# Attention and SwiGLU on one core: from pairs of heads over 112 keys to fours of heads over 64 keys, and a first batch in two passes

## The chip, the cores and the metric

The kernel runs on one core of one Trainium2 chip. The metric is the device time of one execution in microseconds (us). Shown are the median of three runs of the kernel before, and one further execution that was taken by the hardware profiler. A core has five engines that each work through their own list in order: TensorE (PE in the profile, with its weight loads as PEld), VectorE (DVE), ScalarE (ACT), GpSimd (POOL) and SyncE (SP). PE writes to PSUM[...].

## The reference

Attention over 8 batches, 12 heads, 448 tokens and head width 64, then a SwiGLU block over the 3584 tokens with width 768 and inner width 1536. All inputs and the output are fp32; the kernel works in fp16 with fp32 sums.

```python
scores = (q @ k.transpose(0, 1, 3, 2)) / 8.0          # 8 x 12 x 448 x 448
attn = softmax(scores)                                # over the keys
x = (attn @ v).transpose(0, 2, 1, 3).reshape(3584, 768)
g = x @ w_gate
out = (g * sigmoid(g) * (x @ w_val)) @ w_out          # 3584 x 768
```

## The kernel before, in words

**Attention.** The unit is a pair of heads, 48 pairs in all, six to a batch. A token index is split as four tokens a partition over 112 partitions (`P = 112`, `NC = 4`), so that a load moves runs of four tokens. `load_qk16` and `load_v` bring q, k and v in through POOL's DMA queue, which casts fp32 to fp16 on the way; pair 0 comes as fp32 through SP's queue (`load_qk32`). q and k must be turned so that the head width lies on the partitions. `prep` does that in two ways: for pairs under `NPE = 11` PE turns them (L208) and DVE copies the result (L209), and from pair 11 on POOL reorders (L167) and SP issues DMA transposes (L170, L174).

`qk(pr, c)` makes the scores of one chunk of 112 keys: two matmuls of 64 contraction rows and 128 columns, one per head, each over 448 queries (L217), which sit in the upper and the lower half of the array's rows. ACT takes the exponential of both heads at once, 112 x 896 numbers (L225). `pv_chunk` multiplies the exponentials with v, which carries a column of ones so that the sums of the softmax come along: 8 matmuls of 112 rows, 128 columns and 65 moving columns a chunk (L243, L251), 32 a pair. DVE divides (L262, L264), and `turn_x` turns the result into the layout of the next block, on PE for pairs under `XPE = 12` (L291, then L298 on DVE), by DMA afterwards (L300, L304). The last 64 queries of a batch are turned together in `turn_rests` (L310).

**Feed-forward.** A batch is a block of 384 or 512 tokens. `ffn1_steps` has 12 steps a block: six matmuls for the gate (L326 into `gp`), a tanh on ACT (L341), six matmuls for the value (`vp`), and two DVE operations (L345, L348). `ffn2_steps` has steps of 12 matmuls with 384 moving columns (L371), an ACT copy (L378) and the stores (L390). All weights are loaded once and stay in SBUF.

**Order.** The whole order is written out by hand under `tc.manual_schedule()`. A start stage runs the first `FIRST = 6` pairs, batch 0, to the end with little else beside them. Then a list of visits, `plan`, interleaves: each visit has the scores of two or three chunks, the products of at most one or two pairs, and some feed-forward steps of the batch that was finished before. `wq` says at which pair the weight loads are put into POOL's list, between the loads of q, k and v: `wg`, `wv` in four slices each, then `wo` in two halves. PSUM is split into three tiles of two banks (`ps_s`, scores and gates) and two banks (`ps_f`, everything else).

Of the kernel before, what the change touches and what calls it, by code (L numbers as in the profile page):

```python
# [16 lines left out]
HS = 4096.0  # L17
NB = 2
GP = 3
NPE = 11  # L20
LA = 6
RB = 5
FIRST = 6
WIDE = 8
XPE = 12
NE = 4
NX = 6
NV = 5
VS = 9
EB = 15  # L30
# [3 lines left out]
def kernel(  # L34
# [14 lines left out]
    P = 112  # L49
    NC = S // P  # L50
# [4 lines left out]
    NGRP = NPAIR // GP  # L55
    GPB = NHP // GP
    sm_scale = float(D) ** -0.5
    OH = DM // 2
    MQ = S - D
# [13 lines left out]
    load_table("exp_and_others")  # L73

    consts = ctx.enter_context(tc.tile_pool(name="consts", bufs=1))
    raws = ctx.enter_context(tc.tile_pool(name="raws", bufs=2))
# [5 lines left out]
    ps_f = ctx.enter_context(tc.tile_pool(name="ps_f", bufs=2, space=PSUM))  # L82

    Es = [consts.tile([P, NC * EB + 1, D], FP16, name=f"E{i}") for i in range(NE)]
    Xts = [consts.tile([128, 7, D], FP16, name=f"xt{i}") for i in range(NX)]
    Xrs = [consts.tile([D, 128], FP16, name=f"xr{i}") for i in range(3)]
    Vts = [consts.tile([P, 2, NC, D + 2], FP16, name=f"vo{i}") for i in range(NV)]
    vraw = consts.tile([P, VS, 2, NC, D], FP16, name="vraw")
# [11 lines left out]
    wo = [consts.tile([128, NFB, OH], FP16, name=f"wo{i}") for i in range(2)]  # L100
# [5 lines left out]
    def dummy(n):  # L106
        wp = ps_f.tile([128, 512], FP32, tag="f", name="wp")
        for _ in range(n):
            nc.tensor.matmul(wp[:], lhsT=warm[:, 0:128], rhs=warm[:], start=True, stop=True)  # L109

    def load_qk32(pr):
        rq = raws.tile([P, 2, NC, D], FP32, tag="rq", bufs=RB)
        rk = raws.tile([P, 2, NC, D], FP32, tag="rk", bufs=RB)
        for dst, src in ((rq, q), (rk, k)):
            nc.sync.dma_start(dst[:], src[0, 2 * pr : 2 * pr + 2].rearrange("h (p c) d -> p h (c d)", c=NC))
        raw[pr] = (rq[:], rk[:])

    pairbuf = []

    def load_qk16(pr, n=2):  # L120
        h0 = 2 * (pr % 2) if pr >= 14 else 0
        if h0 == 0:
            q16 = raws.tile([P, 4, NC, D], FP16, tag="rq", bufs=RB, name="q16")
            k16 = raws.tile([P, 4, NC, D], FP16, tag="rk", bufs=RB, name="k16")
            pairbuf[:] = [q16, k16]
        q16, k16 = pairbuf
        for dst, src in ((q16, q), (k16, k)):
            flat = src.rearrange("b h s d -> (b h) s d")[2 * pr : 2 * pr + 2 * n]
            nc.gpsimd.dma_start(dst[:, ds(h0, 2 * n)], flat.rearrange("h (p c) d -> p h (c d)", c=NC))  # L129
        for i in range(n):  # L130
            h = h0 + 2 * i
            raw[pr + i] = (q16[:, h : h + 2], k16[:, h : h + 2])

    def load_v(pr, n=1):
        b, h = divmod(2 * pr, H)
        nc.gpsimd.dma_start(  # L136
            vraw[:, ds(pr % VS, n)].rearrange("p r h c d -> p (r h) (c d)"),
            v[b, h : h + 2 * n].rearrange("h (p c) d -> p h (c d)", c=NC),
        )

    def copy_v(pr):
        nc.vector.tensor_copy(Vts[pr % NV][:, :, :, 0:D], vraw[:, pr % VS])  # L142

    def load_w(kind, i):
        if kind == "o":
            src = moe_w_out[:, ts(i, OH)].rearrange("(f p) m -> p f m", p=128)
            dst = wo[i]
        else:
            src = (moe_w_gate if kind == "g" else moe_w_val)[:, ts(i, DF // 4)].rearrange(
                "(t a p) m -> t p a m", p=128, t=2  # L150
            )
            for t in range(2):
                nc.gpsimd.dma_start(wgv[kind, i][:, ts(t, NCB // 2), :], src[t])
            return
        nc.gpsimd.dma_start(dst[:], src)

    def prep(pr):
        rq, rk = raw[pr]
        if pr == 0 or pr >= NPE:
            qk16 = attp.tile([P, 2, NC, 2, D], FP16, tag="qk16", bufs=3)  # L160
            for t, src in enumerate((rq, rk)):
                dst = qk16[:, 1 - t].rearrange("p c h d -> p h c d")
                if pr == 0:
                    nc.vector.tensor_copy(dst[:, 0], src[:, 0])
                    nc.scalar.activation(dst[:, 1], src[:, 1], AF.Copy)
                else:
                    nc.gpsimd.tensor_copy(dst, src)  # L167
        qkT[pr] = attp.tile([128, 2 * S + D], FP16, tag="qkT", name="qkT", bufs=5)
        if pr >= NPE:
            nc.sync.dma_start_transpose(  # L170
                qkT[pr][:, 0 : 2 * S].rearrange("p (c q) -> p c q", q=P),
                qk16[:].rearrange("p t c h d -> p (t c h d)"),
            )
            nc.sync.dma_start_transpose(  # L174
                qkT[pr][:, 2 * S :].rearrange("p (c q) -> p c q", c=1),
                qk16[0:D, 1, 0].rearrange("p h d -> p (h d)"),
            )
            return None

        def turn0():  # L180
            for t in range(2):
                tp = ps_s.tile([128, 2, 512], FP32, tag="s", name="tp")
                for c in range(NC):
                    for hx in range(2):
                        nc.tensor.matmul(
                            tp[ts(hx, 64), c // 2, ds(c % 2 * P, P)],
                            lhsT=qk16[:, 1 - t, c, hx],
                            rhs=ident[0:P, 0:P],
                            start=True,
                            stop=True,  # L190
                        )
                dst = qkT[pr][:, ts(1 - t, S)].rearrange("p (a x) -> p a x", a=2)
                nc.vector.tensor_copy(dst[:, 0], tp[:, 0, 0 : 2 * P])
                nc.scalar.activation(dst[:, 1], tp[:, 1, 0 : 2 * P], AF.Copy)
                if t == 0:
                    tq = tp
            nc.vector.tensor_copy(qkT[pr][:, 2 * S :], tq[:, 0, 0:D])

        def turn():
            if pr < FIRST + 2:  # L200
                tp = ps_s.tile([128, 2, 1024], FP16, tag="s", name="tp")[:, 0]
            else:
                tp = ps_f.tile([128, 1024], FP16, tag="f", name="tp")
            for i in range(2 * NC + 1):
                t, c = (1 - i // NC, i % NC) if i < 2 * NC else (0, 0)
                for hx in range(2):
                    src = raw[pr][t][:, hx, c, :]
                    nc.tensor.transpose(tp[ts(hx, 64), ts(i, P)], src, ident[0:P, 0:P])  # L208
            nc.vector.tensor_copy(qkT[pr][:], tp[:, 0 : 2 * S + D])  # L209

        return turn if pr else turn0

    def qk(pr, c):
        t = qkT[pr]
        s = ps_s.tile([128, 2, 512], FP32, tag="s")
        for hx in range(2):
            nc.tensor.matmul(  # L217
                s[:, hx, 0:S],
                lhsT=t[ts(hx, 64), c * P : c * P + 128],
                rhs=t[ts(hx, 64), ds(S + (1 - hx) * D, S)],  # L220
                start=True,
                stop=True,
            )
        e = Es[pr % NE][:, ds(c * EB, 16)].rearrange("p (h b) x -> p h (b x)", h=2)
        nc.scalar.activation(e[:, :, 0:S], s[0:P, :, 0:S], AF.Exp, scale=sm_scale)  # L225

    def qk_half(pr, half, between=None):
        for c in (2 * half, 2 * half + 1):
            qk(pr, c)
            if between and c % 2 == 0:  # L230
                between()
# [3 lines left out]
    def pv_chunk(pr, c):  # L235
        if c == 0:
            accs[pr] = ps_f.tile([128, 512], FP32, tag="f", name="acc")
        e = Es[pr % NE]
        vo = Vts[pr % NV]
        a7 = accs[pr][:, 0 : 7 * (D + 1)].rearrange("p (s d) -> p s d", s=7)  # L240
        for j in range(3):
            for hx in range(2):
                nc.tensor.matmul(  # L243
                    a7[:, 2 * j + hx],
                    lhsT=e[:, ds(c * EB + 9 * hx + 2 * j, 2)].rearrange("p b x -> p (b x)"),
                    rhs=vo[:, hx, c, 0 : D + 1],
                    start=c + j + hx == 0,
                    stop=False,
                )
        for hx in range(2):  # L250
            nc.tensor.matmul(  # L251
                a7[:, 6],
                lhsT=e[:, ds(c * EB + 6 + hx, 2)].rearrange("p b x -> p (b x)"),
                rhs=vo[:, hx, c, 0 : D + 1],
                start=False,
                stop=c == NC - 1 and hx == 1,
            )
# [384 lines left out]
```

The softmax here doesn't subtract the row's maximum and nothing guards it: scores larger than these inputs give would overflow.

## Time and profile before

| what | us |
|---|---|
| median of three runs (453.3 to 453.51) | 453.31 |
| the profiled execution's own time | 453.5 |
| its span on the core | 451.7 |
| first feed-forward matmul starts | 29.79 |
| PE busy | 441.9 |
| ACT busy | 238.8 |
| DVE busy | 201.6 |
| POOL busy | 141.8 |

The profiled execution's time is 1.8 us more than its span, which runs from the first to the last instruction, and 0.2 us above the median of the runs. A busy PE is not PE at its peak: matmuls overlap, and the record of one holds its latency. So the groups of PE are read by the distance from one start to the next.

### The profile page before, as it was taken

The page shows a single profiled execution, that of the slowest core. Times are in us where ns is not written, and L with a number is a line of the kernel's source. Part 1 is how long each engine was busy: PE and PEld are TensorE (multiplying, and loading weights), DVE is VectorE, ACT ScalarE, POOL GpSimd, SP SyncE. Part 2 cuts the span into 40 slices and gives each one's busy share as a digit, 9 for nine tenths or more (in the row PEclk, how much of TensorE's full clock was granted, in tenths as well). Part 3 has the DMA queues.
Part 4 walks back from the last instruction along what each step waited for, and adds up shares of the span by engine and source line. Part 5 has one row for each costly group of instructions (what it writes and reads, how often), then busy time and mean ns, then how long its engine had stood idle before and what let it go on. Part 6 is the DMA issues. An engine that isn't in the chain of part 4 may idle for free.

```text
span 451.7 us, 9871 instructions
## 1 busy us (share of the span) xinstructions
PE 441.9 (98%) x4024; PEld 247.0 (55%) x4024; DVE 201.6 (45%) x447; ACT 238.8 (53%) x350; POOL 141.8 (31%) x228
## 2 busy tenths in 40 slices
PE   8999999999999999999999999999999999999995
PEld 3655565545455556454555656545455666544563
DVE  3666562456654434455443534353453544055300
ACT  6965666566746465554554546644555462222221
POOL 8755715927642225252313405330100000000000
PEclk9999999999999999999999999999999999999999
DMA  9999999999969379874749758772503112200033
GB/s 142 173 200 201 196 172 174 180 209 119 145 93 133 46 129 124 132 120 71 126 74 120 98 78 143 118 105 68 101 20 68 46 46 57 70 2 0 17 100 95
DMA packets 105101, 48.71 MB, mean 108 GB/s; under 512 B 59744, under 2 KB 101600, under 8 KB 105056
## 3 DMA queue, kind: packets, MB, share of 16 engines
q0 software_dynamic: 43392, 23.37, 41.2%
q1 hardware_dynamic: 61664, 24.71, 28.9%
q8 instruction: 31, 0.51, 0.5%
q14 instruction: 14, 0.11, 0.1%
HBM read 47.19 MB, written 11.01 MB: 129 GB/s over the span
## 4 chain that ended last, share of the span: by engine, by line
PE 93%; DVE 3%; ACT 2%; issue 1%; DVEq 0%; ACTq 0%
PE op L371 24%; PE gp L326 23%; PE vp L326 23%; PE s L217 9%; PE acc L243 9%; PE acc L251 2%; ACT E L225 2%; PE tp L208 1%; PE wp L109 1%; DVE t L345 1%; ACT sg L341 1%; DVE qkT L209 0%; DVE xt L264 0%; PE acc L291 0%; DVE hts L348 0%
## 5 line engine op out<-in xcount | busy, mean ns | idle before, releaser
L225 ACT ACTIVATE E<-s 112x896 f16<-112x896 f32 x192 | 162.1, 919 | 27.5 <-PE s L217 27.4
L326 PE MATMUL gp<-X,wg 128*128 128x384 f16 (+1 forms) x576 | 124.7, 352 | 0.0
L326 PE MATMUL vp<-X,wv 128*128 128x384 f16 (+1 forms) x576 | 124.6, 352 | 0.0
L371 PE MATMUL op<-wo,hts 128*128 128x384 f16 (+1 forms) x684 | 116.1, 323 | 0.0
L345 DVE SCALAR_TENSOR_TENSOR t<-sg,gp 128x384 f32<-128x384 f32 (+1 forms) x96 | 59.7, 621 | 121.8 <-ACT sg L341 121.8
L341 ACT ACTIVATE sg<-gp 128x384 f32<-128x384 f32 (+1 forms) x96 | 52.5, 547 | 84.8 <-PE gp L326 83.6
L371 PEld LDWEIGHTS <-hts 128*128 128x128 f16 x684 | 65.5, 98 | 45.9 <-issue 3.9
L326 PEld LDWEIGHTS <-wv 128*128 128x128 f16 x576 | 56.3, 98 | 52.6
L326 PEld LDWEIGHTS <-wg 128*128 128x128 f16 x576 | 53.1, 97 | 45.6 <-issue 1.1
L378 ACT ACTIVATE osb<-op 128x384 f32<-128x384 f32 (+1 forms) x57 | 27.8, 487 | 92.5 <-PE op L371 92.5
L167 POOL COPY qk<-q 112x512 f16<-112x512 f16 x37 | 22.9, 619 | 144.5 <-DMA qkT<-qk 143.1
L348 DVE SCALAR_TENSOR_TENSOR hts<-t,vp 128x384 f16<-128x384 f32 (+1 forms) x96 | 59.6, 621 | 10.0
L243 PEld LDWEIGHTS <-E 112*128 112x128 f16 x1152 | 46.7, 97 | 18.2 <-issue 17.5
L243 PE MATMUL acc<-vo,E 112*128 112x65 f16 x1152 | 53.0, 193 | 1.3 <-DVE vo L142 0.7
L217 PE MATMUL s<-qkT 64*128 64x448 f16 x384 | 50.6, 355 | 0.2
L251 PE MATMUL acc<-vo,E 112*128 112x65 f16 x384 | 42.9, 193 | 0.0
L262 DVE RECIPROCAL R<-acc 128x7 f32<-128x7 f32 x48 | 9.8, 205 | 70.6 <-PE acc L251 70.5
L129 POOL DMA_DIRECT2D k<-in_k_dram x44 | 29.0, 660 | 9.5 <-DMA wo<-in_moe_w_out_dram 7.8
L129 POOL DMA_DIRECT2D q<-in_q_dram x44 | 29.3, 666 | 5.2 <-PE s L217 2.5
L136 POOL DMA_DIRECT2D vraw<-in_v_dram x42 | 28.0, 666 | 8.4 <-DVE vo L142 7.2
L217 PEld LDWEIGHTS <-qkT 64*128 64x128 f16 x384 | 14.5, 94 | 25.8 <-issue 18.6
L264 DVE TENSOR_TENSOR xt<-acc,R 128x384 f16<-128x384 f32 (+1 forms) x48 | 27.6, 574 | 1.7
(41 smaller groups left out, 148.2 us busy)
## 6 DMA issues: line engine op xcount, KB each, us to landing
q<-in_q_dram POOLq DMA_DIRECT2D x41, 112.0 KB, 4.0
k<-in_k_dram POOLq DMA_DIRECT2D x41, 112.0 KB, 4.6
vraw<-in_v_dram POOLq DMA_DIRECT2D x39, 112.0 KB, 4.6
wg<-in_moe_w_gate_dram POOLq DMA_DIRECT2D x8, 288.0 KB, 10.1
wv<-in_moe_w_val_dram POOLq DMA_DIRECT2D x8, 288.0 KB, 10.2
wo<-in_moe_w_out_dram POOLq DMA_DIRECT2D x2, 1152.0 KB, 22.0
out_dram<-osb SPq DMA_DIRECT2D x8, 288.0 KB, 3.0
out_dram<-osb SPq DMA_DIRECT2D x8, 240.0 KB, 3.1
```

The costliest lines, as they stand in the source:

```text
L129: nc.gpsimd.dma_start(dst[:, ds(h0, 2 * n)], flat.rearrange("h (p c) d -> p h (c d)", c=NC))
L136: nc.gpsimd.dma_start(vraw[:, ds(pr % VS, n)].rearrange("p r h c d -> p (r h) (c d)"), v[b, h : h + 2 * n].rearrange("h (p c) d -> p h (c ...
L217: nc.tensor.matmul(s[:, hx, 0:S], lhsT=t[ts(hx, 64), c * P : c * P + 128], rhs=t[ts(hx, 64), ds(S + (1 - hx) * D, S)], start=True, stop=True,)
L225: nc.scalar.activation(e[:, :, 0:S], s[0:P, :, 0:S], AF.Exp, scale=sm_scale)
L243: nc.tensor.matmul(a7[:, 2 * j + hx], lhsT=e[:, ds(c * EB + 9 * hx + 2 * j, 2)].rearrange("p b x -> p (b x)"), rhs=vo[:, hx, c, 0 : D + 1] ...
L251: nc.tensor.matmul(a7[:, 6], lhsT=e[:, ds(c * EB + 6 + hx, 2)].rearrange("p b x -> p (b x)"), rhs=vo[:, hx, c, 0 : D + 1], start=False, st ...
L326: nc.tensor.matmul(dst[:, 0:n], lhsT=wslice(kind, fb, cb), rhs=X[kk][:, cb, ds(c0, n)], start=(cb == 0), stop=(cb == NCB - 1),)
L341: nc.scalar.activation(sg[:, 0:n], gp[:, 0:n], AF.Tanh, scale=0.5)
L345: nc.vector.scalar_tensor_tensor(t1[:, 0:n], sg[:, 0:n], 1.0, gp[:, 0:n], ALU.add, ALU.mult)
L348: nc.vector.scalar_tensor_tensor(hts[:, fb, 0:n], t1[:, 0:n], 0.5 * HS, vp[:, 0:n], ALU.mult, ALU.mult)
L371: nc.tensor.matmul(op[:, 0:w], lhsT=hts[:, fb, ts(ch, 128)], rhs=wo[oh][:, fb, ds(m0 - oh * OH, w)], start=(fb == 0), stop=(fb == NFB - 1),)
L378: nc.scalar.activation(osb[:, ds(m0, w)], op[:, 0:w], AF.Copy, scale=1.0 / HS)
```

## The change

Almost all of the attention part is rewritten; the feed-forward arithmetic is not.

- **Layout.** Seven tokens a partition over 64 partitions (`NT = 7`). The unit of loading and of scores is a four of heads (`P`, two pairs); k lies in partitions 0 to 63 and q in 64 to 127, so a DMA covers 64 partitions with runs of 1792 bytes. The first four comes as fp32 through the queues of SP and ACT.
- **Scores.** `score(P, t, ta, tb)` makes 64 keys by up to 448 queries for four heads: four matmuls of 64 rows and 64 columns, one in each quarter of the array, then one exponential of 128 x 896. There are 7 a four instead of 8 chunks for two pairs.
- **Products.** `pv_piece` uses 64 rows and 128 columns; the two heads of a pair lie in the two row halves and write different PSUM banks. There are 7 x 4 x 2 = 56 matmuls a pair, in 28 twos, with 65 moving columns. `pv_close` divides, in two parts a pair except for the first six and the last two pairs.
- **Turning.** `turn` has 28 transposes of 64 x 64 a pair, on PE for pairs under 14; the later ones take one POOL copy and one DMA transpose a pair (`prep`). `turn_x` stays on PE up to pair 17; `turn_rests` is gone.
- **Batch 0 in two passes.** In the start stage only the first 256 queries of batch 0 are scored and multiplied, in an order given by the string `START`. The other 192 follow in the first visits. The feed-forward of batch 0 and 1 is cut into blocks of 256, 384 and 256 tokens; the first runs while the rest of batch 0 and all of batch 1 go through attention.
- **Loads.** All weight loads and the first loads of q, k and v are put into POOL's list up front, in the order shown below; later loads come at the visit where a four enters, three or four fours ahead.

```diff
-NPE = 11
-FIRST = 6
-XPE = 12
+NPE = 14
+TA = 4
+FIRST = 6
+XPE = 18
+START = "sssdststsvsv" "sspppstsppps" "tsxsx" "vvsspppsvvspppsxpsxsppppp" "xx"
...
+    def load_qk(P):
+        raw[P] = raws.tile([128, 4, NT * D], FP16, tag="qk", name="qk")
+        nc.gpsimd.dma_start(raw[P][0:64], heads(k, 4 * P, 4))
+        nc.gpsimd.dma_start(raw[P][64:128], heads(q, 4 * P, 4))
...
+    def prep(p):
+        st = attp.tile([128, NT, 2, D], FP16, tag="st", name="st", bufs=3)
+        src = raw[p // 2][:, ts(p % 2, 2)].rearrange("p h (t d) -> p t h d", t=NT)
+        nc.gpsimd.tensor_copy(st[:], src)
+        new_qkT(p)
+        nc.sync.dma_start_transpose(
+            qkT[p][:].rearrange("p t a q -> p t (a q)"), st[:].rearrange("p t h d -> p (t h d)")
+        )
...
+    def score(P, t, ta, tb):
+        s = stile("s")
+        n = (tb - ta) * D
         for hx in range(2):
-            nc.tensor.matmul(
-                s[:, hx, 0:S],
-                lhsT=t[ts(hx, 64), c * P : c * P + 128],
-                rhs=t[ts(hx, 64), ds(S + (1 - hx) * D, S)],
-                start=True,
-                stop=True,
-            )
+            for i in range(2):
+                T = qkT[2 * P + i]
+                nc.tensor.matmul(
+                    s[ts(hx ^ i, 64), hx, 0:n].rearrange("p (t q) -> p t q", q=D),
+                    lhsT=T[ts(hx, 64), t, 0],
+                    rhs=T[ts(hx, 64), ta:tb, 1],
+                    start=True,
+                    stop=True,
+                )
...
+        for t in tset:
+            for j, slot in enumerate(slots):
+                for hx in range(2):
+                    c = ts(hx ^ (p % 2), 64)
+                    n[hx] += 1
+                    nc.tensor.matmul(
+                        banks[hx][:, ts(j, D + 1)],
+                        lhsT=E[p // 2, t][c, ds(hx * S + slot * 128, 128)],
+                        rhs=Vts[p % NV][c, t, 0 : D + 1],
+                        start=n[hx] == 1,
+                        stop=n[hx] == NT * len(slots),
+                    )
...
+    BL = [(0, 0, 256), (0, 256, 384), (0, 640, 256)]
+    for b in range(2, B):
+        BL.append((b // 2, 384, 512) if b % 2 else (b // 2, 0, 384))
...
+        load_qk(1)
+        make_identity(nc, ident)
+        load_v(0)
+        load_qk(2)
+        load_v(1)
+        load_v(2)
...
+        for i in range(2):
+            load_w("g", i)
+            load_w("v", i)
+        for i in range(2, 4):
+            load_qk(i + 1)
+            load_v(i + 1)
+            load_w("g", i)
+            load_w("v", i)
...
+        load_qk(5)
+        load_v(5)
+        load_qk(6)
+        load_v(6)
+        load_w("o", 0)
+        load_w("o", 1)
+        load_qk(7)
+        load_v(7)
+        load_w("o", 2)
+        load_w("o", 3)
...
+        for p in range(FIRST, NPE):
+            pre.setdefault(entry[p // 2] - 2 + p % 2, []).append(p)
+        for P in range(NPE // 2, NQ):
+            for i in range(2):
+                pre.setdefault(entry[P - 2] + i, []).append(2 * P + i)
+        loads = {}
+        for P in range(8, NQ):
+            loads.setdefault(entry[P - 4], []).append((load_qk, P))
+            loads.setdefault(entry[P - 3], []).append((load_v, P))
```

## The prediction

> **What bounds the kernel now.** I read the page first (busy shares, slices, chain), then the groups, then the timeline of PE in one steady visit and at the end of the start stage, and last the DMA side of the first 75 us.
>
> ```profile
> PE 441.9 (98%) x4024; PEld 247.0 (55%) x4024; DVE 201.6 (45%) x447; ACT 238.8 (53%) x350; POOL 141.8 (31%) x228
> ...
> DMA  9999999999969379874749758772503112200033
> ...
> PE 93%; DVE 3%; ACT 2%; issue 1%; DVEq 0%; ACTq 0%
> ...
> L225 ACT ACTIVATE E<-s 112x896 f16<-112x896 f32 x192 | 162.1, 919 | 27.5 <-PE s L217 27.4
> ```
>
> PE is busy for 98% of the span and holds 93% of the chain that ended last. No other engine comes near, but the DMA row stands at 9 for the first eleven slices (124 us).
>
> A steady visit on PE (start, length, group):
>
> ```profile
> 142.44 0.74 PE L217 MATMUL s<-qkT 64*128 64x448 f16 x6
> 143.11 0.36 PE L243 MATMUL acc<-vo,E 112*128 112x65 f16 x6
> ...
> 144.09 1.14 PE L326 MATMUL gp<-X,wg 128*128 128x384 f16 x6
> 145.06 1.14 PE L326 MATMUL vp<-X,wv 128*128 128x384 f16 x6
> ```
>
> From start to start: six score matmuls take 0.67 us, though three times 448 columns at the rate of the feed-forward (0.162 us for 384) are only 0.57. So the two matmuls of a chunk already run side by side in the two row halves (single starts in the trace lie 3 ns apart), 0.190 us a chunk, and 0.10 is left over. In single starts this rest is 94 to 98 ns wherever the shape of the array's tiles changes, and nothing where it doesn't: 258 ns instead of 162 from feed-forward to scores, 281 instead of 187 from scores on, but 29 from products to feed-forward. The products take 0.98 us for 32 matmuls, 30.4 ns each.
>
> The end of the start stage:
>
> ```profile
> 28.43 0.22 PE L251 MATMUL acc<-vo,E 112*128 112x65 f16 x2
> 29.61 0.34 PE L291 MATMUL acc<-ident,xt 128*128 128x128 f16 x3 [0.96 <-DVE xt L264]
> 29.79 1.14 PE L326 MATMUL gp<-X,wg 128*128 128x384 f16 x6
> ```
>
> Feed-forward begins at 29.8. Until then ACT sets the pace: 26 exponentials of 0.806 us (2.53 for three, 0.92 of one). From 29.8 on I count 413.2 us of PE work (rates below) and see 416.6 to the last matmul's end: only 3.4 us of waits. 5.3 us follow for the last copy and store.
>
> The input stream (busy time by engine, clock, DMA share, GB/s written; then the landing times of `qkT` in 48 to 73 us, and over the whole run):
>
> ```profile
> 33.90:45.20 11.30, 10.91 (x136) 6.75 (x133) 7.52 (x16) 6.64 (x9) 6.59 (x9) 1.00 1.35 201
> ...
> DMA to landing us min/median/max: 9.2/11.1/14.5
> ...
> DMA to landing us min/median/max: 2.3/4.4/14.5
> ```
>
> The stream is full at about 200 GB/s of fp16, twice that read: weight transfers of 288 KB land 1.45 us apart (407 GB/s read), q and k of 112 KB 0.60 apart (382). Weights are all there at 50.6, needed by about 60. While `wo` streams, a DMA transpose takes 11 us instead of 4.4. The kernel before hides this by a margin of some 10 us.
>
> **What the Trainium skill says.** "TensorEngine Tiling (Array Packing)", Key Properties: changing the tiling mode drains PE. The trace agrees, about 95 ns. "TensorE: Matmul & The Clock Gate", Part 3, The mechanism: matmuls of different tiles start about 4 ns apart and overlap. Agrees: 3 ns in L217, and in the transposes of L310 (64 moving columns, two column tiles) two per 31.6 ns. "SBUF — State Buffer", The DMA port swizzle: 64 partitions reach half of the DMA ports, about 196 to 218 GB/s written. No trace here shows it; 200 GB/s is the rate wanted, so I expect no gain and a small loss from the new layout.
>
> **The change part by part, PE.** Rates in ns: columns/2.4 + 2.4 for the feed-forward (162 and 216 fit), 95 a change of mode. Before: first feed-forward 576 x 162.4 + 576 x 215.7 = 217.8; second 109.2; products 1536 x 30.4 = 46.7; scores 192 x 190 = 36.5; turns 98 twos x 49.3 = 4.8; x-turns and rests 2.4; warm-up 2.6; 172 changes of mode 16.3. Sum 436.3.
>
> After, counted in the order of its instructions:
> - First feed-forward: 288 x 109.1 (256 columns) + 576 x 162.4 + 432 x 215.7 = 218.1. Second 109.2.
> - Scores: 147 full units x 190 + 21 split in 256 and 192 columns (110 + 84) = 32.0. Gain 4.5. Four quarter tiles at once are not in the trace; two are. If only two overlap, it costs 32 more; if all do, this stands. I take four.
> - Products: 2688 in 1344 twos. A two in row halves with 65 columns isn't shown; L310's 31.6 and the 30.4 of a single one bound it: 41.0 (39.4 to 42.5). Gain 5.7. If the twos didn't overlap: 81.7, a loss of 35.
> - Turns: 14 pairs x 28; in fours of 31.6 it is 0.22 us a pair, in twos 0.44; I take 0.31, 4.4. X-turns 3.5 (54 x 55.7 + 18 x 29).
> - Changes of mode: 197, because the products now differ from the feed-forward that follows: 18.7, 2.4 more.
> - Warm-up 2.4. Sum 429.3, gain **7 us**. Pre-feed-forward work is 12.9 of it (22.9 before), so 416.5 comes after.
>
> **The start.** ACT has 21 exponentials of 512 numbers, about 0.48 each (0.806 less 384 numbers at 0.86 ns, from L341's 0.49 and 0.60): 10.1 us. The first starts later, near 7.8 (before 6.6): the first load is twice as large and the fp32 copies of the second pair stand in DVE's and ACT's order ahead of the first turn's. With 1.5 of gaps, closing, x-turn and the first scores: feed-forward at about 21.4. Were all else as before: 21.4 + 416.5 + 3.4 + 5.3 = 446.6, 5 us faster.
>
> **What is late next: the input.** Attention now runs ahead of feed-forward: block 0 has 256 tokens and is spread over 15 visits with all of batch 1. PE's work from the first feed-forward matmul to the turn of pair 10 is 17.8 us, and to the first scores of four 7 (pairs 14, 15) 37.5: due at 39.2 and 58.9. Before, the scores of pair 14 start at 84.8.
>
> The stream, from 4.2 (first four landed): up to four 5, q, k, v are 3.44 MB at about 415 GB/s read (extrapolated from 382 at 512-byte and 407 at 768-byte packets to 896), 16.6 us; weights 4.72 MB, 23.2; interruptions 2.1, as before lost between 14 and 24 us. Four 5 lands at **46.1**, 7 late for pair 10's turn, which stands in PE's order before everything else. Then v5, four 6, v6, half of `wo` and four 7: 12.5 more, 58.6. Its POOL copies (1.1 each) and SP's transposes follow: the second is issued at 60.8 and lands 4.4 to 11.1 later, 65.2 to 71.9, while the second half of `wo` streams. Due with the first wait included: 65.8. I take the middle, **68.5**. PE, and ACT and DVE behind it, stand still meanwhile; nothing covers it.
>
> Sum: 68.5 + 379.0 (416.5 - 37.5) + 2 (the later part of the 3.4) + 5.3 = 454.8 of span, against 451.7. With 1.8 around the span and 0.2 off for the median: **456.4**.
>
> Costed at nothing: POOL's reorder copies and SP's single transpose later on (POOL is 31% busy, and the stream drains after `wo`); DVE's two-part division (two reciprocals of 0.2 and two products of about 0.42 instead of 0.2 + 0.6 + 2 x 0.28 in most pairs), hidden behind feed-forward. In the visits from 18 to 42 us after the first feed-forward matmul DVE has about 22 us of 24: cover thin there, 0 to 3 us. The products take both banks of `ps_f`, so their second matmul waits for whoever had the newer one; mostly an ACT copy of 0.49, against 0.76 of scores ahead. 0 to 2 us.
>
> **Rivals.** *The input is in time* (ends faster): if the transposes land as in the quiet part (pair 15 at 64) and the stream runs at 430 instead of 410 GB/s, pair 10 waits 4 instead of 7 and pair 14 next to nothing more: 62 + 379 + 7.3 = 448.3 span, 450 run; with no wait at all 448.2. It decides for faster once the first scores of four 7 start before 64. For it: the runs of 1792 bytes are longer than any before. Against: the weights come at 407 with half the bytes. *Packing pays less*: fours that run as twos, or DVE and bank waits in every visit, add 5 to 35: 460 to 490. Against: all two-tile cases in the trace overlap fully. *The change doesn't do what it says*: were the row tiles of the products serial, the profile would show 30 ns instead of 15 a product; the last case holds this.
>
> **How the numbers follow.** Late input 0.68 (452 to 461), input in time 0.2 (447 to 452), packing pays less 0.12 (460 and up). This kernel's measurement can tell about 0.2% (0.9 us) from no change: of the first case 0.09 falls within it and 0.01 is faster; of the second 0.01 within. Faster 0.2, same 0.1, slower 0.7. Range 449 to 464: it takes in most of the second case and the near part of the third.
>
> **What would show it.** Right: feed-forward starts at 20 to 23; L165 waiting for `qk` DMAs in 25 to 47, L185 for `qkT` transposes in 60 to 72, 7 to 12 us in all; 190 ns from score unit to unit, 30 a two of products; 95 ns at each change. Wrong: PE without gaps in 22 to 72 (then about 448), score units at 380, or waits for DVE in every visit.

## The result, and the profile after

The changed kernel takes **479.16 us** (median of four runs, 477.85 to 480.42), the kernel before 453.41 (four runs on the same chip): a ratio of 1.0567, 95% interval 1.0534 to 1.0600. It is slower, as forecast, but by 25.8 us instead of 3.1, and outside the range. The profiled execution took 480.42, with a span of 478.3.

The lines of the page after that answer to those of before (engines, slices of the span, instruction queue, chain, exponentials):

```profile
PE 451.8 (94%) x5899; PEld 267.5 (56%) x5899; DVE 212.8 (44%) x528; ACT 224.5 (47%) x359; POOL 104.8 (22%) x154
PE   5789777999999999999999999999999999999996
PEclk8759999799999999999999999999999999999999
DMA  9999999864164399956583877554131012220033
q8 instruction: 46, 0.75, 0.7%
PE 85%; ACT 7%; issue 2%; DVE 2%; DMA 2%; ACTq 0%; SPq 0%; DVEq 0%
```

The row `PEclk` is the granted clock, the speed at which PE was let run, in tenths of full. PE has 5899 matmuls instead of 4024, and the loss stands in the first seven slices (84 us), where its row reads 5789777 and not 8999999. From the eighth on it reads 9 as before. The seven lie within the stretch in which the DMA row reads 9. The list that PE works through comes in over the queue `q8`: 46 packets of 16 KB instead of 31.

A steady visit late in the kernel (start, length, group) shows the rates of the prediction to be right:

```profile
223.59 0.76 PE L185 MATMUL s<-qkT 64*64 64x448 f16 x12
224.28 1.03 PE L217 MATMUL f<-vo,E 64*128 64x65 f16 x56
225.24 1.47 PE L291 MATMUL gp<-X,wg 128*128 128x512 f16 x6
```

Three score units take 0.69 us from start to start (190 ns each and 0.1 for the change of mode), 28 twos of products 0.96 (30.9 ns each and 0.095). So the packing does pay what was counted. The time is lost at the front, in three stretches (columns: window, busy time of the engines, granted clock, DMA share, GB/s written):

```profile
11.60:32.20 20.60, 16.23 (x395) 10.03 (x394) 10.12 (x28) 12.37 (x25) 12.77 (x19) 0.67 1.30 202
32.20:93.00 60.80, 50.41 (x1168) 35.67 (x1164) 33.56 (x100) 38.84 (x64) 28.00 (x41) 0.92 1.21 180
93.00:474.50 381.50, 379.42 (x4284) 219.73 (x4276) 165.98 (x372) 169.53 (x268) 55.69 (x78) 1.00 0.47 78
```

The first score starts at 11.6, the first feed-forward matmul at 32.2, the first one of a block of 384 tokens at 93.0. By the prediction's own rates the middle stretch holds 41.1 us of PE work and took 60.8. What PE waited for in it (waiting group, releaser, us in total, times, longest):

```profile
PE s L185 <- ACT E L194: 2.8, 9, 0.4
PE f L217 <- issue: 2.0, 2, 1.7
PE tp L165 <- ACT E L194: 1.9, 4, 0.6
PE gp L291 <- ACT E L194: 1.6, 4, 0.4
PE tp L165 <- issue: 1.5, 1, 1.5
```

No wait for an input transfer is among them, which was the prediction's cause. There are two others: waits for exponentials, which free the three score tiles (`ps_s`, in PSUM, where the matmuls of this kernel write their results), and "issue", where nothing in the profile holds PE. Those last stand in the middle of a run of equal instructions, with no semaphore near them:

```profile
69.06 0.41 PE L165 MATMUL tp<-ident,qk 64*64 64x64 f16 x27
70.99 0.19 PE L165 MATMUL tp<-ident,qk 64*64 64x64 f16 x1 [1.52 <-issue]
...
81.53 0.90 PE L217 MATMUL f<-vo,E 64*128 64x65 f16 x47
84.16 0.45 PE L217 MATMUL f<-vo,E 64*128 64x65 f16 x9 [1.72 <-issue]
```

Counted from the start of the program, five such stops of 0.3 to 1.7 us all fall at matmul 94 or 95 of a group of 128. A matmul is two instructions (weight load and multiply), so that is one stop for 256 instructions; 16 KB for 256 is 64 bytes each. The sizes agree: 46 packets of 256 are 11776 instructions, and PE has 2 x 5899 = 11798. In the trace the packets of `q8` lie mostly 5.8 to 6.5 us apart from 17 to 88 us, with two gaps of 7.0 and 8.5 (17.0, 22.9, 28.9, 35.9, 44.4, 50.6, 56.6, 62.4, 68.6, 75.1, 81.6, 88.0).

**Theories.** A, *instruction supply*: while the DMA engines are full, PE gets 256 instructions only every 6 us, and row and column tiles need half as many again, most densely at the front. B, *clock*: PE runs at half clock in part of the front (0.67 on average in the start), and that stretches the work. C, *ring*: three score tiles and ACT's 0.81 us an exponential set the pace of the visits. D, *first load*: POOL's stream shares the DMA engines with the first four, whose second half landed only at 9.4. And the recorded one, *late input*.

### The profile page after: what moved, and what is told of

The parts are those of the page before. It is cut to its first block, busy times and chain, and to the rows that moved or that the text cites. A ratio compares the mean times of both kernels' runs of the same rounds, so it can differ in the third digit from the quotient of the medians.

```text
span 478.3 us, 13524 instructions
## 1 busy us (share of the span) xinstructions
PE 451.8 (94%) x5899; PEld 267.5 (56%) x5899; DVE 212.8 (44%) x528; ACT 224.5 (47%) x359; POOL 104.8 (22%) x154
## 4 chain that ended last, share of the span: by engine, by line
PE 85%; ACT 7%; issue 2%; DVE 2%; DMA 2%; ACTq 0%; SPq 0%; DVEq 0%
PE f L291 23%; PE f L333 23%; PE gp L291 22%; PE f L217 7%; PE s L185 7%; ACT E L194 6%; DMA raw<-in_k_dram 2%; PE acc L217 1%; PE xtp L260 1%; ACT osb L340 1%; DVE t L310 1%; PE tp L165 1%; ACT sg L306 0%; DVE xt L241 0%; DVE h L313 0%
## 5 line engine op out<-in xcount | busy, mean ns | idle before, releaser
L194 ACT ACTIVATE E<-s 128x896 f16<-128x896 f32 (+2 forms) x189 | 144.0, 839 | 25.8 <-PE s L185 25.7
L291 PE MATMUL f<-X,wv 128*128 128x384 f16 (+2 forms) x648 | 128.1, 335 | 0.2 <-DVE t L310 0.2
L291 PE MATMUL gp<-X,wg 128*128 128x384 f16 (+2 forms) x600 | 119.3, 335 | 2.3 <-ACT E L194 2.3
L333 PE MATMUL f<-wo,h 128*128 128x384 f16 (+1 forms) x684 | 115.6, 323 | 0.2 <-DVE t L310 0.2
L306 ACT ACTIVATE sg<-gp 128x384 f32<-128x384 f32 (+2 forms) x100 | 51.0, 510 | 101.3 <-PE gp L291 98.2
L310 DVE SCALAR_TENSOR_TENSOR t<-sg,gp 128x384 f32<-128x384 f32 (+2 forms) x100 | 57.3, 573 | 81.9 <-ACT sg L306 81.7
L333 PEld LDWEIGHTS <-h 128*128 128x128 f16 x684 | 66.3, 98 | 44.6 <-issue 1.5
L291 PEld LDWEIGHTS <-wg 128*128 128x128 f16 x648 | 60.7, 99 | 47.0 <-issue 4.7
L313 DVE SCALAR_TENSOR_TENSOR h<-t,f 128x384 f16<-128x384 f32 (+2 forms) x108 | 61.5, 569 | 12.7 <-DVE t L310 0.9
L185 PE MATMUL s<-qkT 64*64 64x448 f16 (+2 forms) x756 | 51.0, 353 | 3.6 <-ACT E L194 2.9
L217 PE MATMUL f<-vo,E 64*128 64x65 f16 x2408 | 47.1, 190 | 2.3 <-issue 2.0
L185 PEld LDWEIGHTS <-qkT 64*64 64x64 f16 x756 | 19.9, 109 | 28.6 <-issue 22.9
## 6 DMA issues: line engine op xcount, KB each, us to landing
wo<-in_moe_w_out_dram POOLq DMA_DIRECT2D x4, 576.0 KB, 10.9
```

What stands on the lines that cost most here:

```text
L185: nc.tensor.matmul(s[ts(hx ^ i, 64), hx, 0:n].rearrange("p (t q) -> p t q", q=D), lhsT=T[ts(hx, 64), t, 0], rhs=T[ts(hx, 64), ta:tb, 1], s ...
L194: nc.scalar.activation(e[:, 0 : 2 * S].rearrange("p (h q) -> p h q", h=2)[:, :, ds(ta * D, n)], s[:, :, 0:n], AF.Exp, scale=sm_scale,)
L217: nc.tensor.matmul(banks[hx][:, ts(j, D + 1)], lhsT=E[p // 2, t][c, ds(hx * S + slot * 128, 128)], rhs=Vts[p % NV][c, t, 0 : D + 1], start ...
L291: nc.tensor.matmul(dst[:, 0:n], lhsT=wslice(kind, fb, cb), rhs=X[kk][:, cb, ds(c0, n)], start=(cb == 0), stop=(cb == NCB - 1),)
L306: nc.scalar.activation(sg[:, 0:n], gp[:, 0:n], AF.Tanh, scale=0.5)
L310: nc.vector.scalar_tensor_tensor(t1[:, 0:n], sg[:, 0:n], 1.0, gp[:, 0:n], ALU.add, ALU.mult)
```

## The experiments

### The supply by itself

A kernel with nothing but 2304 twos of products from constant tiles, and loads beside them:

```python
for i in range(2304):
    for hx in range(2):
        c = ts(hx, 64)
        nc.tensor.matmul(acc[:, hx, 0:65], lhsT=E[c, 0:128], rhs=vo[c, 0:65],
                         start=i == 0, stop=i == 2303)
```

> The disputed resource by itself: PE issues 4608 products of 64 rows, 128 columns and 65 moving columns, two row halves alternately, from memory that is set once, with no wait of any kind in the stream; meanwhile POOL's queue brings in wg and wv twice and wo once (23.6 MB of fp32, about 58 us at 407 GB/s read), after which the DMA engines are quiet. It computes nothing of the reference: its output is not attention or feed-forward. Instruction supply (PE's list comes in pieces of 256 instructions, 128 matmuls, and a piece takes about 6 us while the DMA engines are full): while the weights stream the products stop after each 128 and advance by about 128 in 6 us, with the waits put down to issue; when the stream is over they advance at least twice as fast. Rival (the matmuls or their waits set the pace in the changed kernel, the gaps at each 128 are chance): 15 ns a product throughout, 128 in 2 us, all 4608 done in about 72 us, no difference between the loaded and the quiet part.

Measured: the slices of PE and of DMA, then the timeline while the loads run, then after them.

```profile
PE   7927644276536885565476456645954761000000
...
DMA  4999999999999200000000000000000002999996
```

```profile
20.59 3.48 PE L70 MATMUL acc<-vo,E 64*128 64x65 f16 x128 [2.22 <-issue]
26.51 3.27 PE L70 MATMUL acc<-vo,E 64*128 64x65 f16 x128 [2.44 <-issue]
32.43 2.12 PE L70 MATMUL acc<-vo,E 64*128 64x65 f16 x128 [2.65 <-issue]
38.35 3.71 PE L70 MATMUL acc<-vo,E 64*128 64x65 f16 x128 [3.80 <-issue]
...
73.22 2.12 PE L70 MATMUL acc<-vo,E 64*128 64x65 f16 x128 [1.61 <-issue]
76.95 2.12 PE L70 MATMUL acc<-vo,E 64*128 64x65 f16 x128 [1.61 <-issue]
80.41 2.12 PE L70 MATMUL acc<-vo,E 64*128 64x65 f16 x128 [1.34 <-issue]
```

There are bursts of exactly 128 products, one every 5.92 us while the loads run and, in the lines shown, every 3.5 to 3.7 us when nothing else moves. So a product costs 46 ns and 28 ns here instead of the 15 at which it runs. The stops came as expected; the gain after the loads did not reach the forecast, 1.6 to 1.7 times as fast and not twice. The bursts at half clock (3.48 and 3.71 us long) and the one at full clock (2.12) begin at the same distance: in this stream, which the supply holds, the clock costs nothing.

The second stream has the loads on SP's queue, without the cast, at 371 to 401 GB/s:

```diff
-                        nc.gpsimd.dma_start(w[:, ts(t, NCB // 2), :], s[t])
+                        nc.sync.dma_start(w[:, ts(t, NCB // 2), :], s[t])
```

> The stream of 4608 products again (nothing of the reference is computed), with the loads put on SP's queue as plain fp32 (wg, wv, wo once, 14.2 MB, about 35 us at 400 GB/s) instead of POOL's casting queue. If a full set of DMA engines is what makes PE's list slow, whichever queue fills it, 128 products again take about 6 us until the loads are in, then 3.6. If it is the casting queue, or POOL's descriptors, 128 products take 3.6 to 4 us from the start.

Measured: bursts at 14.40, 20.87, 27.34 and 33.54, so 6.2 to 6.5 us for 128, then 3.7 to 4.0 from 46.91 on.

```profile
20.87 3.70 PE L70 MATMUL acc<-vo,E 64*128 64x65 f16 x128 [2.77 <-issue]
27.34 3.71 PE L70 MATMUL acc<-vo,E 64*128 64x65 f16 x128 [2.77 <-issue]
```

PE's list comes slowly beside full DMA engines, whichever of the two queues fills them; POOL's casting queue is not needed for it.

### The visits: supply against ring

First attempt at quiet DMA engines, weights set by POOL:

```diff
-            nc.gpsimd.dma_start(wo[:, ts(i, NFB // 4)], src[:, ts(i, NFB // 4)])
+            nc.gpsimd.memset(wo[:, ts(i, NFB // 4)], 0.0)
```

> The changed kernel without its weight loads (wg, wv, wo are set to 0 by POOL instead, so the feed-forward result is all zero; every PE, ACT and DVE instruction stays). Instruction supply: with DMA engines that are free half of the time, instruction fetches lie 2 to 4 us apart instead of 6 between 17 and 88 us, the issue gaps at each 128 matmuls vanish, first feed-forward starts 2 to 5 us earlier and the visits up to 93 us lose 8 to 12 us less: 460 to 466 in all. Ring of three score tiles and ACT's pace: the stage from first feed-forward to 93 us keeps its length (60 us) apart from what starts earlier: 472 to 479. Late input as the prediction had it: would give back its 10 us too, but then PE's waits in the kernel after would have been for qk loads and qkT transposes, which they were not.

Measured: median 470.44, ratio 1.0376 (1.0343 to 1.0410). The profiled execution is one of 493.06, over 20 us above the other four (470.0 to 472.5): in it DVE's second cast took 21.2 us beside POOL's memsets, after 0.39 for the first (10.8 is their mean). Its visits took 54.9 us. As a test of the start it is void, so it was made again without the memsets:

```diff
-        return wgv[kind, i][:, cb, ds(off, 128)]
+        return zw[:, 0:128]          # one tile of zeros for all weights
```

> The changed kernel again without its weight loads, this time with no work put in their place: one tile of 128 x 384 zeros stands for all of wg, wv and wo, so the feed-forward result is zero; all PE, ACT and DVE instructions and waits stay. (The run with POOL's memsets held DVE's two first copies for 10.8 us each and so told little of the start.) First scores start near 11.6 as in the changed kernel. Instruction supply is all of the loss: no waits put down to issue, first feed-forward at 22 to 25 instead of 32.2, the visits up to the first block of 384 in 45 us instead of 60.8: about 453 in all. Supply and the ring of three score tiles share it (what the run with memsets showed from first feed-forward on: 54.9 us for these visits): first feed-forward at 26 to 30, then 55, then as before: 464 to 470. Ring alone: 475 to 479.

Measured: 474.56, ratio 1.0457 (1.0437 to 1.0478). No issue wait is left in the visits, which took 55.3 us instead of 60.8; the start stayed at 20.6 (10.9 to 31.5). There the run is no test of supply: q, k and v alone still moved 202 GB/s from 15 to 30 us, and PE ran at half clock all the while.

Then the ring, by halving ACT's work in the first 16 visits:

```diff
+        m = 1 if short[0] else 2
-            s[:, :, 0:n],
+            s[:, 0:m, 0:n],
```

> Weights stay. In the first 16 visits ACT takes the exponential of one head of each two, 128 x 448 instead of 128 x 896, and the products of both heads read that half, so the values of batch 0's later queries and of batch 1 are wrong; PE's instructions and waits are the same. It takes away about 0.37 us of 0.81 from each of some 60 exponentials. Ring of three score tiles, freed by ACT: the waits of scores, xtp, tp and gp for ACT vanish in the visits and these get 8 to 9 us shorter, 469 to 472 in all. Instruction supply alone: PE then waits for its list instead, at the same 6 us for each 128 matmuls, and the total falls by 0 to 2: 477 to 479. Both in series, each hiding behind the other: 3 to 5 us less, 474 to 476.

Measured: 478.86, ratio 1.0550 (1.0528 to 1.0572); visits 60.1 us. The waits for ACT nearly went, and the time stood up again as issue:

```profile
PE f L221 <- issue: 4.9, 3, 2.6
PE tp L165 <- issue: 2.8, 2, 1.5
PE s L187 <- ACT E L198: 1.0, 3, 0.5
```

And both at once:

> Both at once: no weight loads (feed-forward result zero) and half exponentials in the first 16 visits (see the two runs before). If supply and ring are the whole loss of the visits, these come near PE's counted work of 41.1 us (43 to 47 instead of 60.8), and the total is that of the run with zero weights less 7 to 10: 455 to 460. If something else holds them (DVE's divisions and turns, the two banks of ps_f), they stay above 50.

Measured: 470.27, ratio 1.0360 (1.0336 to 1.0385); visits 50.1 us, with two waits left in the view:

```profile
PE s L174 <- ACT E L185: 1.0, 3, 0.5
PE s L174 <- DVE X L258: 0.4, 1, 0.4
```

| first feed-forward to first block of 384, us | exponentials whole | halved |
|---|---|---|
| DMA engines full | 60.8 | 60.1 |
| no weight loads | 55.3 | 50.1 |

This is the table of two limits side by side, each hiding behind the other: the ring alone is worth 0.7, the loads alone 5.5, both 10.7. Of the 19.7 us above the counted work 9.0 remain with both taken away. The clock has a small part in these numbers. The changed kernel is at half clock from 32.2 to 35.3 and from 83.1 to 89.9 us, the last run up to 36.3 only. At half clock six matmuls of 256 columns take 1.26 to 1.42 us from start to start and not 0.66 to 0.74; from that, and the work that lies there, I estimate 3 us of the 19.7 and 2 of the 9.0. The other 7 were not split further.

On B these runs say nothing, though their page seems to: it puts the mean clock of the last two at 0.996 and 0.999 instead of 0.971. In their traces the first record of the clock lies at 36.1 and 36.3 us, and the products tell what it was before. Two runs of 28 in the changed kernel, where the clock is recorded as full and as half, and one in the last run:

```profile
16.00 0.61 PE L217 MATMUL acc<-vo,E 64*128 64x65 f16 x28
22.48 0.95 PE L217 MATMUL acc<-vo,E 64*128 64x65 f16 x28
...
24.40 0.95 PE L208 MATMUL acc<-vo,E 64*128 64x65 f16 x28 [0.17 <-DVE xt L232]
```

In both runs the start's products are of the longer kind throughout, so both starts went at half clock. The test of B comes with the start below.

A smaller piece of the ring, the first gate of each early visit in a bank of `ps_f`:

```diff
-            gate_small[0] = bare
+            gate_small[0] = bare or x < 16
```

> The first gate of each of the first 16 visits goes into a bank of ps_f instead of a score tile: one user of the ring of three fewer in each visit, nothing else changed. Ring: gp's waits for ACT (2.3 us in the profile) go and tp and scores wait less, 2 to 4 us less in all, 475 to 477. Instruction supply: no change within 0.3%, 478 to 480, with the time turning up as issue.

Measured: 482.12, ratio 1.0636 (1.0601 to 1.0671). That lies above both forecasts. The visits of the profiled execution took 59.6, 1.2 less, and issue grew from 3.5 to 3.9; its clock stayed full after 34.5 us, which by itself could account for the 1.2. The times show no gain, in line with the table: the ring alone gives next to nothing.

### The start

> Load of pair of fours 1 moved behind the identity and the 17 memsets of the E pads, which go from DVE to POOL, so that POOL's stream starts 2 to 3 us later and shares less with the first four's fp32 load; and 14 dummy matmuls instead of 1 between the two first turns, so that PE doesn't idle while it waits. Late first load and half clock: the second half of the first four lands at 7 to 8 instead of 9.4, first score at 8 to 9.5 instead of 11.6, full clock up to about 20 us, first feed-forward at 27 to 29 instead of 32.2, in all 4 to 6 us less, 473 to 475. Instruction supply: first score comes earlier, but the pieces still take 6 us each once the stream runs, so that first feed-forward starts at 30 to 31 and the total falls by 1 to 3: 476 to 478.

```diff
-        load_qk(1)
         make_identity(nc, ident)
+        for e in Es:
+            nc.gpsimd.memset(e[:, 2 * S :], 1.0)
+        load_qk(1)
...
-        dummy(1)
+        dummy(14)
```

Measured: 479.69, ratio 1.0571 (1.0508 to 1.0634). The second half of the first four landed at 7.8 instead of 9.4, but the 14 dummies took 4.4 us and held the second turn until 10.8; first score 11.65. That is inconclusive for D, but it tests B. With the dummies the clock is recorded as full from 8.9 to 26.0 us, and 28 products take 0.60 to 0.61 us there. B had the first feed-forward at 27 to 29. It came at 31.64, 20.0 us after the first score instead of 20.6. PE stopped longer for its list, at these two places:

```profile
18.23 0.26 PE L165 MATMUL tp<-ident,qk 64*64 64x64 f16 x9 [0.96 <-issue]
24.43 0.27 PE L185 MATMUL s<-qkT 64*64 64x256 f16 x1 [1.74 <-issue]
```

In the changed kernel the stops stand at 19.25 (1.72) and 25.18 (0.49), before products. With 13 more dummies ahead they stand at other instructions, and again at place 95 of 128. So some 10 us more of full clock were worth 0.6 us from the first score on, and B is small.

For D, once more without the dummies:

> The change of the run with clock and first load, without its dummies: load of four 1 behind the identity and the memsets of the E pads, which POOL does instead of DVE; one dummy between the first two turns, as in the changed kernel. In that run the first four's second half landed at 7.8 instead of 9.4, but 14 dummies held PE until 10.8. So the first score is expected at 9.8 to 10.3 instead of 11.6. If the start is a chain of its own (turns, exponentials, divisions), all 1.5 us reach the first feed-forward (30.5 to 31) and the total (477). If instruction supply sets the pace from 16 us on, at 6 us for each 128, it reaches neither: first feed-forward at 31.5 to 32.2, total 478 to 480.

Measured: 479.55, ratio 1.0578 (1.0562 to 1.0593). The first score starts at 9.9, 1.7 us earlier, and the first feed-forward at 30.7, 1.5 earlier. Then the visits take 62.6 instead of 60.8, and the first block of 384 starts at 93.3 instead of 93.0. The issue waits in the visits grew from 3.5 to 5.6 us. What was gained by reaching the visits early was lost in them: D is real and worth nothing here.

Last, the start with quiet DMA engines: zero weights, and POOL waits with four 3 and later until START's last x-turn:

```diff
+        nc.gpsimd.tensor_copy(gate[:, 0:8], X[0][:, 5, 0:8])
+        load_qk(3)
+        load_v(3)
```

> Zero weights as before, and the loads of q, k and v from four 3 on wait until START's last x-turn is copied (one POOL copy of 8 columns that reads it), so that the DMA engines are quiet from about 15 us, while everything before the first feed-forward is the same. (The feed-forward result is zero.) If PE's list makes the start long, its pieces come at up to one in 3.6 us, the issue waits in START (2.2 us in the changed kernel) go, and the first score to first feed-forward takes 14 to 17 us instead of 20.6. If START's own chain does (one accumulator, each pair's division and x-turn before the next, ACT idle between), it stays at 19 to 20.6.

Measured: 470.61 in one run. First score to first feed-forward:

```profile
10.93 1.02 PE L173 MATMUL s<-qkT 64*64 64x256 f16 x12
...
28.37 2.33 PE L279 MATMUL f<-X,zw 128*128 128x256 f16 x12
```

17.4 us, between the two expectations, and 3.2 less than the 20.6 of the run with both reliefs, whose first score starts at about the same time. Not all of the 3.2 is supply. 1.1 of it arises before the second pair's products: there that run has a stop of 1.08, again at place 95 of 128, and this one has none. The other 2.1 arises after them, where this run has full clock (from 18.6 us on) and that one half. So quiet DMA engines and full clock together are worth 3.2; the run with the dummies shows that the clock alone gives little, and quiet engines at an unchanged clock were not run. No issue wait remains. What does remain is START's own order: 21 exponentials at 0.53 to 0.54 us, pauses of ACT between them of 0.2 to 0.6 us and 2.1 at the end, while PE stands at products and x-turns behind DVE's divisions. This is read from the waits; the order itself was changed in no run:

```profile
PE xtp L248 <- DVE xt L229: 0.9, 2, 0.7
PE acc L205 <- DVE xt L229: 0.7, 2, 0.4
```

### Parts of the change

One pass over batch 0:

```diff
-TA = 4
+TA = 7
-    BL = [(0, 0, 256), (0, 256, 384), (0, 640, 256)]
+    BL = []          # 384 and 512 a batch, from batch 0 on
```

> The two passes of batch 0 undone alone: START scores all 448 queries of batch 0 (21 exponentials of 0.81 us), its products and turns follow whole, feed-forward blocks are 384 and 512 tokens as before; row and column tiles, layout and loads stay. Instruction supply: PE has the same number of attention instructions before the end of batch 1 but 288 matmuls fewer of feed-forward in the whole kernel and more work for each instruction in the first visits, so fewer stalls: first feed-forward later (38 to 42), visits faster, total 462 to 472. Ring and ACT's pace: batch 0 in the start stage is bound by ACT, first feed-forward at 36 to 38, the ring's waits in the first visits go (second-pass units are gone), total 460 to 470. Recorded prediction (packing gains, only the input is late): 455 to 460. Above 479 would mean that the two passes were worth their price.

Measured: 473.02, ratio 1.0422 (1.0405 to 1.0440). First feed-forward starts at 43.2. From there to 110 us the waits above counted work are about 10 us. So the second pass cost about 6 us: it brings feed-forward 11 us forward, and more than that is lost again afterwards, presumably in visits that hold attention and one thin feed-forward step each. The time lies above the bands of both theories, so it favours neither.

Fewer instructions for PE:

```diff
-NPE = 14
+NPE = 10
```

> NPE = 10 instead of 14: pairs 10 to 13 are turned by a POOL copy and a DMA transpose as the later pairs are. PE issues 112 matmuls (224 instructions) fewer between 60 and 75 us, and four users of the ring of three score tiles go. Instruction supply and ring hiding each other: both are relieved at once, so the visits up to the first block of 384 get 3 to 5 us shorter (56 to 58 instead of 60.8), 474 to 476 in all. Input as the recorded prediction had it: the DMA transposes run while wo streams, take 9 to 15 us each, and pair 10 comes late, so 479 to 484. Neither: 478 to 480.

Measured: 492.36, ratio 1.0860 (1.0822 to 1.0898). This miss is instructive:

```profile
PE s L185 <- DMA qkT<-st: 10.7, 2, 6.7
PE s L185 <- ACT E L194: 5.2, 10, 1.1
```

The first two transposes came up on SP at 55.1 and 56.5 and landed at 68.7 and 76.0, 13.6 and 19.5 us later. Here is the wait that the prediction expected. It is there, one step behind: with `NPE = 14` the four pairs that would meet it are turned on PE.

The three reliefs together:

> One pass over batch 0, the first load placed as in the run before the last, and NPE = 10: the three edits that relieve the start, the ring and PE's list. One pass alone gave 473.0, with first feed-forward at 43.2 and 11 us of waits up to 110 us. If the gains add, 1 to 2 us from the first load and 2 to 4 from the turns: 467 to 470. If the transposes come late or PE's list still sets the pace, 471 to 474. None of the theories expects it to reach the kernel before (453).

Measured: 484.19, ratio 1.0691 (1.0643 to 1.0738), with 15.4 us of waits for those transposes. No version here comes near the kernel before, and none of the runs points to one: with the weights left out and the exponentials halved it is still 16.5 us behind.

## Why the prediction was wrong, point by point

The prediction's span and the measured one, by the stretches of its own steps:

| stretch | forecast | measured | difference |
|---|---|---|---|
| to the first exponential | 7.8 | 12.2 | 4.4 |
| first exponential to first feed-forward | 13.6 | 20.0 | 6.4 |
| from there to the first block of 384 | 50.7 | 60.8 | 10.1 |
| the rest | 382.7 | 385.3 | 2.6 |
| span | 454.8 | 478.3 | 23.5 |

The third forecast is 41.1 of counted work and 9.6 of waiting for four 7.

**The rates were right.** 190 ns a score unit, 30.9 a two, 95 a change of mode; after 93 us there are 381.2 us to the last matmul's start, for 375.4 counted. The 95 ns at a change of tiling mode and the overlap of the tiles agree with the two sections of the Trainium skill that the prediction drew on. For loads on 64 partitions "SBUF — State Buffer", The DMA port swizzle, has about 196 to 218 GB/s written. The start moved 202, but that is no test of it: the weights in this stream cover 128 partitions, and the kernel before moved 201 over 112. The prediction named as signs of error score units at 380, waits for DVE in every visit, or a PE without gaps. None came. The sign that did come was not on its list.

**"First feed-forward at about 21.4" failed.** It took ACT's exponentials as the only pace. The 10.8 us are three terms. 4.4 come before the first exponential: the first four's second half lands at 9.4, with POOL's loads on the same engines (an earlier turn for this load took off 1.7). 3.2 went with quiet DMA engines and full clock together. The last 3.2 stayed even then. The exponential of 512 numbers was put at 0.48 and measured 0.53 to 0.54, which for 21 of them makes 1.2 us; the likely rest is START's order over DVE, which was not tested, and half clock up to 18.6 us in that run.

**"PE stands still for the input" failed, though its landing times of the loads held.** (It counts its megabytes as fp16 and its rate as fp32 read; 16.6 us is what comes out when both are fp32.) The q of four 5 landed at 48.2 (forecast 46.1), that of four 7 at 60.7 (58.6). But PE turned pair 10 at about 57.6 and scored four 7 at 87.6, not at 39.2 and 58.9 as it would have without waits. A late transfer costs only what it is later than its reader, and the reader was late itself. The run with `NPE = 10` shows that the mechanism exists and that 15.4 or 10.7 us of it lay within reach. The transposes of pairs 14 and 15 landed at 76.9 and 81.6 (68.5 was forecast for the second), 6 us before their reader.

**The step that was left out is the visits' own pace.** Their 60.8 us were sized by PE's work alone. The count of instructions was in the page (8048 before) and in the diff (28 transposes and 56 products a pair), but work was counted in ns and not in instructions: 1168 matmuls in the visits are 9.1 pieces of 256, about 55 us at 6.0 each, against 41.1 us of work. And three exponentials of 0.81 us a visit (2.4), through three score tiles that a turn, an x-turn and a gate use too, are nearly as long as a visit's PE work (41.1 over 15 visits, 2.7), so that neither engine can run ahead of the other. That both limits matter is measured: with the loads gone the visits took 55.3, with the exponentials halved 60.1, with both 50.1. That these two counts are the reason is argued from the numbers, and 9.0 us are explained by neither. The prediction had neither limit.

**The rivals.** "The input is in time" had its premise come true, and ended at 479 instead of 450. "Packing pays less, 460 and up" was nearest in time, but by DVE and bank waits that are not there: packing paid in full. That the row tiles would run one after the other is excluded by 30.9 ns a two.

**In the rest**, 5.8 us above the counted work instead of 2. It is spread out: 0.03 us at each of 33 steps from scores to products (1.0), 1.6 at five steps from an x-turn to a gate, three of them marked as waits for ACT, and 0.8 at one x-turn, also behind ACT. What holds the remainder was not tried.

## What to carry to other kernels

Count PE's work twice, in ns and in instructions: small tiles that overlap halve the first and not the second, and where the DMA engines are full the second can be the longer one. Look for waits put down to "issue" in the middle of a run of equal instructions, and for the distance of the instruction queue's packets; if that distance is constant over stretches with different work, the list itself may be the limit. When two limits lie this close, take both away before calling either one harmless: here the two alone gave 0.7 and 5.5 us, and together 10.7. And hold a mean clock against the length of one kind of matmul before building on it.

## What was not expected of the hardware

- PE's list arrives in pieces of 16 KB, 256 instructions. With the DMA engines full a piece takes 5.9 to 6.5 us, with nothing else on them 3.5 to 4.0. At 28 ns a matmul even quiet DMA engines don't keep up with a stream of matmuls that run at 15.
- The recorded clock can be wrong over a whole stretch: in the two runs with halved exponentials it stands at 9 tenths or more at the front, while 28 products take 0.95 us there, as they do where it is recorded at 0.50, and 0.61 at full. And half clock can cost nothing: in the stream of products bursts of 3.48 and 2.12 us began at the same distance of 5.92.
- The first two DMA transposes beside a full load stream landed 13.6 and 19.5 us after they came up on SP, in the run with `NPE = 10`; the kernel before showed 14.5 at most.
